# Bursts of two P·V visits between score stretches of one row half, with their sums added up on GpSimd

## The chip, the cores and the metric

The kernel runs on one core of a Trainium2 chip. The metric is device time in microseconds (us), the median of three runs; less is better. A core has TensorE (PE: matmuls, with the weight loads shown as PEld), VectorE (DVE), ScalarE (ACT), GpSimd (POOL), SyncE (SP: here it only issues DMAs) and 16 DMA engines. Matmuls write PSUM, which has 8 banks of 128 partitions x 512 fp32. GpSimd doesn't read PSUM in this kernel; ScalarE and VectorE do.

## The reference

```python
def _A_ref(x, wq, wk, wv, wo):              # S=2048, D=640, H=32 heads, Dh=20
    q = (x @ wq).reshape(B, S, H, Dh).transpose(0, 2, 1, 3)
    k = x @ wk                              # one key and value head for all
    v = x @ wv
    scores = jnp.einsum("bhqd,bkd->bhqk", q, k) * (Dh ** -0.5)
    p = softmax(scores, axis=-1)
    o = jnp.einsum("bhqk,bkd->bhqd", p, v)
    return o.transpose(0, 2, 1, 3).reshape(B, S, H * Dh) @ wo
def _B_ref(x, w1, b1, w2, b2):              # token mixing, F=1728
    h = layernorm(x, axis=-1)
    u = gelu(jnp.einsum("bsd,sf->bdf", h, w1) + b1)
    y = jnp.einsum("bdf,fs->bds", u, w2) + b2
    return y.transpose(0, 2, 1)
g = sigmoid((x * gate_w).sum(-1, keepdims=True))
return g * _A_ref(...) + (1 - g) * _B_ref(...)
```

## The kernel before

Most fp32 operands of a product are split in a high and a low part (hi, lo) in the format of the fast matmul, and a product is the sum of hi x hi, hi x lo and lo x hi.

**Attention.** 2048 queries are cut in 4 blocks of 512 and the 32 heads in 8 groups of four: 32 head groups n, each with 16 blocks of 128 keys. One unit u = (n, kb) is a head group and a key block; there are 512. For a unit, `qk` (L625) makes four score tiles s of 128 keys x 512 queries, two of them (pr) on each half b of the array's rows (partitions 0 to 63 or 64 to 127); ScalarE's exp writes each to a tile p (L635). The visit `pv_mm` (L653) then multiplies the unit's four p tiles with the values: four matmuls in four column groups of 32, all 128 rows, summed over the 16 key blocks in one bank o that belongs to a head group. Row 20 of each column group is the sum of p, since v has a column of ones. When the last key block is in, o is transposed, scaled by the inverse of the sums, transposed back (VectorE and GpSimd, the list `later`, one step per phase) and split in hi and lo for o_scr in DRAM.

The exp needs each query's maximum beforehand. So the scores are made a second time with the queries on the partitions: `ms_next` (L454) gives 64 matmuls ms per head group, each with a reduce over 512 keys on VectorE (L469). The maxima go through DRAM (`store_max`, `fetch_max`) into two more rows of the q tile qst. ms reads a q tile of its own, qmx, with the same data; both come from q_scr with six DMAs each (`load_q`).

**Fills.** Everything else of TensorE is put beside it as matmuls of 64 rows x 320 columns into one bank g: W1 of the mixer with its Gelu (`b1_jobs`, L867), W2 (`b2_jobs`, L704), and the output projection of the first eight row tiles (`a_jobs`, L816); the projection of the last eight (L773) fills the end. The weights of W1 and W2 come in chunks of 512 rows x 128: a load on SyncE, then on GpSimd a cast to hi and a subtraction to lo (`w1_upto`, L123 and L124).

**The loop.** In phase k of 488, the row half b = k % 2 gets four s (units k-1 and k) and three or four ms, alternating; the other half gets a batch of fills (9.6 on average with W1, 10.1 with W2, 7 or 8 or 15 in the projection) and at times one ms. `beside` puts the two halves' matmuls in one order by their modelled length, so that the two halves of the array work side by side. Then comes the visit of unit k-1, which needs all rows. W1 takes 180 phases, W2 256, the projection 52. Because the next phase's fills go to the same bank g from the other row half, they wait for a one-element memset on VectorE (`signal`, L645) that follows the last fill. The last 24 units run in `stretch` (L981), with two visits after one another.

Banks in the loop: three for ms (ps_m), three for s (ps_s), one for o (ps_o), one for g (ps_g). The order on each engine is the order in which the program calls the instructions; nothing reorders them.

Of the kernel before, what the change touches and what calls it, by code (L numbers as in the profile page):

```python
# [37 lines left out]
def mix_kernel(ctx: ExitStack, tc: tile.TileContext, A_x, A_wq, A_wk, A_wv, A_wo,  # L38
# [13 lines left out]
    m_scr = dram.tile([NU, P, 32], F32, name="m_scr")  # L52

    ident = const.tile([P, P], F32, name="ident")
    make_identity(nc, ident)
# [19 lines left out]
    qp = ctx.enter_context(tc.tile_pool(name="qp", bufs=2, side="right"))  # L75
# [53 lines left out]
    def load_q(n, name):  # L129
        t = qp.tile([P, 2, NB], F32R, name=name)  # L130
        qb, g = divmod(n, NQ)
        cols = slice(qb * NB, (qb + 1) * NB)

        def part(b, j, src):
            o = 64 * b + DH * j
            rows = q_scr[src, g * 4 * DH:(g + 1) * 4 * DH, cols]
            nc.sync.dma_start(out=f32(t[o:o + DH]), in_=rows.rearrange("(a b d) q -> b d a q", a=2, b=2)[b])
# [9 lines left out]
    qtiles, qmax = {}, {}  # L147
    one_by_one, q_parts_due = [False], []

    def new_q(n):  # L150
        if n < NU:
            qtiles[n] = load_q(n, "qst")

    def new_qmax(n):
        if n < NU and n not in qmax:
            qmax[n] = load_q(n, "qmx")
# [9 lines left out]
    with tc.tile_pool(name="pa", bufs=1) as pa, \  # L166
            tc.tile_pool(name="tmp", bufs=2) as tmp, \
            tc.tile_pool(name="paw", bufs=2) as paw, \
            tc.tile_pool(name="pxt", bufs=2) as pxt, \
            tc.tile_pool(name="psa", bufs=4, space=PSUM) as psa, \  # L170
            tc.tile_pool(name="pst", bufs=4, space=PSUM) as pst:
        xin = [pa.tile([P, 4, D], F32, name=name) for name in ("xa", "xb")]
# [93 lines left out]
        def x_tiles(sb, c):  # L266
            if sb < 3 and c < 4:
                xT[sb, c] = [spare(sb, c, lo) for lo in range(2)]
            elif sb == 3 and c < 3:
                pair = qp.tile([P, 2, NB], F32R, name=("qst", "qst", "qmx")[c])  # L270
# [118 lines left out]
        for sb in range(NQB):  # L389
# [11 lines left out]
            for m in range(DC):  # L401
# [23 lines left out]
                if sb == 3 and m == 1:  # L425
                    w1_upto(4)
                    new_qmax(0)
# [14 lines left out]
    pp_pool = ctx.enter_context(tc.tile_pool(name="pp", bufs=12))  # L442
    ev = ctx.enter_context(tc.tile_pool(name="ev", bufs=1))
    ps_m = ctx.enter_context(tc.tile_pool(name="ps_m", bufs=3, space=PSUM))
# [4 lines left out]
    row_max = {}  # L449
# [4 lines left out]
    def ms_next(b):  # L454
        k = given[b]
        if k >= 32 * NU:
# [5 lines left out]
        def step():  # L462
            if n not in mtiles:
                mtiles[n] = mpool.tile([P, 16, 4], F32, name="mp")
            ms = ps_m.tile([P, NB], F32, name="ms")
            nc.tensor.matmul(ms, qmax[n][64 * b:64 * b + 60, pr, qt * P:(qt + 1) * P],  # L466
# [4 lines left out]
            if min(issued) == 32 * n + 1:  # L471
                new_qmax(n + 1)
# [13 lines left out]

    def store_max(n):
        mn = row_max[n]
        mt = mpool.tile([P, 32], F32, name="mt")
# [65 lines left out]
    with tc.tile_pool(name="psb", bufs=2, space=PSUM, side="right") as psb:  # L555
# [8 lines left out]
        for fc in range(PRO):  # L564
            pu = [psb.tile([P, NB], F32, name=f"pu{r}") for r in range(2)]
            for hf in range(4):
# [16 lines left out]
                if fc == 1 and hf == 0:  # L583
                    new_q(0)
# [8 lines left out]
    ps_s = ctx.enter_context(tc.tile_pool(name="ps_s", bufs=3, space=PSUM))  # L593
    ps_o = ctx.enter_context(tc.tile_pool(name="ps_o", bufs=1, space=PSUM))
# [7 lines left out]
    def second():  # L602
        right.close()
        pools["rows"] = ctx.enter_context(tc.tile_pool(name="rows", bufs=3, side="right"))

# [17 lines left out]
    odd_s = [0]  # L623

    def qk(u, pr, b):  # L625
        n, kb = units[u]
        if kb == 4 and pr == 0 and b == 0:
            new_q(n + 1)
        q = qtiles[n]
        odd_s[0] ^= 1  # L630
        s = ps_m.tile([P, NB], F32, name="ms") if spare[0] and odd_s[0] and not loaded else ps_s.tile([P, NB], F32, name="s")
# [18 lines left out]
    otile = {}  # L650
    later = []

    def pv_mm(u):  # L653
        n, kb = units[u]
        if kb == 0:
            otile[0] = ps_o.tile([P, NB], F32, name="o")
        o = otile[0]
        for hh in range(4):
            nc.tensor.matmul(o[32 * hh:32 * hh + 32, :], v_sb[:, kb, :], ptiles.pop((u, hh)),  # L659
                             start=(kb == 0), stop=(kb == NS - 1), skip_group_check=True)  # L660
        if kb == NS - 1:
            qb, g = divmod(n, NQ)
            ot = ev.tile([P, NB // 32, 32], F32, name="ot")
            rl = ev.tile([P, NB // 32], F32, name="rl")
            on = ev.tile([P, NB], F32, name="on")
            oh = ev.tile([P, NB], F32R, name="oh")
            ol = ev.tile([P, NB], F32R, name="ol")
            nc.vector.transpose(ot.rearrange("p c e -> p (c e)"), o)

            def scale():  # L670
                nc.vector.reciprocal(rl, ot[:, :, DH])
                (nc.vector if spare[0] else nc.gpsimd).tensor_mul(ot, ot, rl[:, :, None].to_broadcast([P, NB // 32, 32]))

            def back():
                nc.vector.transpose(on, ot.rearrange("p c e -> p (c e)"))

            def high():
                osplit[:] = [oh, ol]
                if n < NU - 1:
                    nc.gpsimd.tensor_copy(oh, on)  # L680
                else:
                    nc.scalar.activation(oh, on, AF.Copy)

            def low():
                (nc.vector if n == NU - 1 else nc.gpsimd).tensor_sub(ol, on, f32(oh))
                for j, t in enumerate((oh, ol) if n < NU - 1 else ()):
                    for hh in range(4):
                        r = (4 * g + hh) * DH
                        nc.sync.dma_start(out=o_scr[j, r:r + DH, qb * NB:(qb + 1) * NB],
                                          in_=f32(t[32 * hh:32 * hh + DH, :]))  # L690

            later.extend((None, scale, back, high, low))

    def b2_jobs(st):
# [22 lines left out]
        def steps(d):  # L717
            full = [[(fc, k), (fc, k)] for fc in range(FC - 1) for k in range(3)]
            return [[lambda fc=fc, k=k, h=h: mm(fc, k, d, h) for h, (fc, k) in enumerate(f)]
                    for f in full + [[(FC - 1, 0), (FC - 1, 1)], [(FC - 1, 2)]]]  # L720
# [41 lines left out]
    def tail_job(n):  # L762
# [4 lines left out]
        def mm(c, k, d, h, first, last):  # L767
            if first:
                acc[d, h] = (ps_g.tile([P, NB], F32, name="g") if h and not d
                             else ps_m.tile([P, NB], F32, name="ms"))  # L770
# [82 lines left out]
    def b1_jobs(d, fc):  # L853
# [19 lines left out]
        return load, [([[lambda h=h, st=st, k=k: mm(st, k, h) for h in range(2)]  # L873
# [16 lines left out]
    k_tail = len(units) - TAIL  # L890
    todo = [divmod(i, FC) for i in range(PRO, 2 * FC)]
    seq = batches([b1_jobs(*t) for t in todo], [5] * len(todo))
    for i, (steps, rest, done) in enumerate(seq):
        item, j = divmod(i + 1, 5)
        rest.insert(0, lambda c=4 * (PRO + item) + (48 * j // 5) // 12: w1_upto(c + 4))
    b2 = [b2_jobs(st) for st in range(NS)]
    m = len(seq)
    seq += batches(b2, [4] * 2 * NS)
    for st in range(NS - 1):
        for j, n in ((1, 1), (2, 2), (3, 4)):  # L900
            seq[m + 8 * st + 4 + j][1].append(lambda c=W2 + 4 * (st + 1) + n: w1_upto(c))
    seq[-1][1].append(second)
    for c in range(DC):
        seq[m + 9 + 8 * c][1].append(lambda c=c: load_wo(c))
        seq[m + 11 + 8 * c][1].append(lambda c=c: split_wo(c))
    aj = [a_jobs(st) for st in range(NS - 8)]
    seq[-8][1].append(aj[0][0])
    twice = k_tail // 2 - len(seq) - 2 * len(aj)
    seq += batches(aj, [2 if i < twice else 1 for i in range(2 * len(aj))])
    ph = [(rows[1 - b], rest if b else [], done if b else []) for rows, rest, done in seq for b in range(2)]  # L910
    assert len(ph) == k_tail
    for i, k in enumerate((443, 451, 459, 467, 473, 477, 481, 485)):
        ph[k][1].append(lambda i=i: tail_load(i))

    X_US, F_US = 0.232, 0.147

    def beside(rows0, rows64, x):
# [143 lines left out]
```

## Time and profile before

| | |
|---|---|
| median of 3 runs | 1698.87 us (1698.53 to 1698.98) |
| profiled execution, span | 1697.4 us |
| DMA | 135.45 MB, 80 GB/s on average |

Busy time of the engines in stretches of 85 us, one of each stage of the loop:

| stage (window, us) | PE | DVE | ACT | POOL | reduces in it |
|---|---|---|---|---|---|
| W1 (340 to 425) | 85.00 | 76.01 | 63.50 | 37.49 | 117 |
| W2 (850 to 935) | 85.00 | 74.88 | 61.46 | 19.23 | 117 |
| projection (1445 to 1530) | 84.96 | 75.28 | 63.80 | 12.37 | 116 |

How to read it: a busy PE only says that some matmul was under way, since matmuls are pipelined and two row halves run at once. What tells is the distance between the starts of neighbouring matmuls. Of the other engines, busy time against the window's length says how far each is from setting the pace; the rows of groups give the busy time, the mean duration of one, and what its engine waited for before.

### The profile page before, as it was taken

How to read it: one execution, taken by the hardware profiler on the slowest of the kernel's cores; microseconds unless marked ns; L12 is line 12 of the kernel's file. 1: busy time of each engine (PE TensorE's matmuls, PEld its weight loads, DVE VectorE, ACT ScalarE, POOL GpSimd, SP SyncE). 2: the span in 40 equal slices, each digit the busy share in tenths (PEclk: the TensorE clock that was granted, in tenths of full speed). 3: DMA queues.
4: the chain of work that ended last, by engine and by line, in shares of the span. 5: the costliest groups of instructions: out<-in, count | busy, mean ns of one | idle time of the engine just before them, and what ended most of it. 6: DMA issues, size and time to landing. Idle time of an engine off the chain costs nothing.

```text
span 1697.4 us, 39056 instructions
## 1 busy us (share of the span) xinstructions
PE 1690.2 (100%) x14865; PEld 1103.0 (65%) x14865; DVE 1435.0 (85%) x2915; ACT 1189.8 (70%) x2322; POOL 570.4 (34%) x723
## 2 busy tenths in 40 slices
PE   9999999999999999999999999999999999999998
PEld 7899766666666666666666666666666666555666
DVE  6679898888888888888888888888888888888734
ACT  4445677777777777777777777777777777777775
POOL 6467644544445454322222212222221111111200
PEclk9999999999999999999999999999999999999999
DMA  7665322222222222121112222212111222344411
GB/s 212 192 177 147 94 64 69 65 64 64 60 69 70 70 70 69 50 64 52 57 49 70 70 60 62 63 56 61 52 52 35 62 63 64 92 113 144 132 57 57
DMA packets 173377, 135.45 MB, mean 80 GB/s; under 512 B 32729, under 2 KB 139382, under 8 KB 173190
## 3 DMA queue, kind: packets, MB, share of 16 engines
q1 hardware_dynamic: 172902, 132.63, 28.0%
q8 instruction: 117, 1.92, 0.5%
q14 instruction: 70, 0.57, 0.1%
q10 hardware_dynamic: 288, 0.33, 0.1%
HBM read 100.27 MB, written 31.65 MB: 78 GB/s over the span
## 4 chain that ended last, share of the span: by engine, by line
PE 96%; issue 2%; DVE 1%; SPq 1%; DMA 0%; POOL 0%; ACT 0%; POOLq 0%; DVEq 0%; ACTq 0%
PE o L659 30%; PE s L632 18%; PE ms L466 17%; PE g L704 12%; PE g L867 8%; PE pp L293 4%; PE pu L576 4%; PE g L816 2%; PE ms L773 1%; PE pt L285 0%; DVE mp L469 0%; PE g L773 0%; DVE st L226 0%; SPq L190 0%; SPq L188 0%
## 5 line engine op out<-in xcount | busy, mean ns | idle before, releaser
L469 DVE TENSOR_REDUCE mp<-ms 128x1 f32<-128x512 f32 x2048 | 1278.4, 684 | 171.1 <-PE ms L466 164.5
L635 ACT ACTIVATE p<-s 128x512 f32<-128x512 f32 x2048 | 1069.1, 603 | 397.4 <-PE s L632 393.8
L466 PE MATMUL ms<-kst,qmx 60*128 60x512 f32 x2048 | 846.8, 421 | 0.9 <-DVE mp L469 0.7
L632 PE MATMUL s<-qst,kst 62*128 62x512 f32 x2048 | 745.1, 404 | 0.0
L659 PE MATMUL o<-p,v_sb 128*32 128x512 f32 x4096 | 554.7, 604 | 0.0
L466 PEld LDWEIGHTS ms<-kst,qmx 60*128 60x128 f32 x2048 | 378.3, 185 | 213.6 <-DVE flag L645 181.1
L632 PEld LDWEIGHTS s<-qst,kst 62*128 62x128 f32 x2048 | 378.2, 186 | 11.5 <-issue 10.9
L867 PE MATMUL g<-slot,wh 64*128 64x320 f32 x1152 | 281.4, 318 | 0.0
L124 POOL TENSOR_TENSOR wl<-wr,wh 128x512 fp32r<-128x512 f32 (+1 forms) x176 | 219.9, 1251 | 35.8 <-ACT wh L121 21.3
L867 PEld LDWEIGHTS g<-slot,wh 64*128 64x128 f32 x1152 | 190.6, 184 | 59.8 <-DVE flag L645 59.8
L123 POOL CAST wh<-wr 128x512 fp32r<-128x512 f32 (+1 forms) x136 | 79.8, 587 | 444.4 <-PE g L704 281.7
L704 PE MATMUL g<-slot,wh 64*128 64x320 f32 x864 | 208.9, 317 | 0.0
L704 PE MATMUL g<-u,wh 64*128 64x320 f32 x864 | 208.8, 317 | 0.0
L659 PEld LDWEIGHTS o<-p,v_sb 128*32 128x32 f32 x4096 | 93.6, 108 | 137.7 <-issue 130.4
L867 PE MATMUL g<-slot,wl 64*128 64x320 f32 x576 | 179.4, 311 | 0.0
L704 PEld LDWEIGHTS g<-slot,wh 64*128 64x128 f32 x864 | 142.3, 184 | 40.2 <-DVE flag L645 40.2
L704 PEld LDWEIGHTS g<-u,wh 64*128 64x128 f32 x864 | 142.3, 184 | 40.2 <-DVE flag L645 40.2
L704 PE MATMUL g<-slot,wl 64*128 64x320 f32 x432 | 135.0, 313 | 0.0
L704 PE MATMUL g<-u,wl 64*128 64x320 f32 x432 | 134.9, 313 | 0.0
L867 PEld LDWEIGHTS g<-slot,wl 64*128 64x128 f32 x576 | 106.1, 184 | 15.1 <-DVE flag L645 15.1
L704 PEld LDWEIGHTS g<-slot,wl 64*128 64x128 f32 x432 | 79.6, 184 | 13.4 <-DVE flag L645 13.4
L704 PEld LDWEIGHTS g<-u,wl 64*128 64x128 f32 x432 | 79.5, 184 | 13.4 <-DVE flag L645 13.4
(195 smaller groups left out, 1404.0 us busy)
## 6 DMA issues: line engine op xcount, KB each, us to landing
wr<-in_B_w_dram SPq DMA_DIRECT2D x152, 256.0 KB
qmx<-q_scr SPq DMA_DIRECT2D x192, 80.0 KB
qst<-q_scr SPq DMA_DIRECT2D x192, 80.0 KB
y_scr<-yo SPq DMA_DIRECT2D x16, 320.0 KB
slot<-o_scr SPq DMA_DIRECT2D x16, 320.0 KB
o_scr<-oh SPq DMA_DIRECT2D x124, 40.0 KB
o_scr<-ol SPq DMA_DIRECT2D x124, 40.0 KB
q_scr<-qh SPq DMA_DIRECT2D x19, 256.0 KB
```

The costliest lines, as they stand in the source:

```text
L123: nc.gpsimd.tensor_copy(wh, wr)
L124: nc.gpsimd.tensor_sub(wl, wr, f32(wh))
L293: nc.tensor.matmul(pp, w, t, start=first and n == 0, stop=not more and n == len(steps) - 1)
L466: nc.tensor.matmul(ms, qmax[n][64 * b:64 * b + 60, pr, qt * P:(qt + 1) * P], kst[64 * b:64 * b + 60, kq * NB:(kq + 1) * NB], start=True, s ...
L469: nc.vector.tensor_reduce(mtiles[n][:, c, kq:kq + 1], ms, axis=AX.X, op=ALU.max)
L576: nc.tensor.matmul(pu[r][:, :HD2], w[rows, c, :], h[rows, st, :], start=(st == 0 and k == 0), stop=(st == NS - 1 and k == 2))
L632: nc.tensor.matmul(s, kst[64 * b:64 * b + 62, kb * P:(kb + 1) * P], q[64 * b:64 * b + 62, pr, :], start=True, stop=True)
L635: nc.scalar.activation(p, s, AF.Exp, scale=SCALE)
L659: nc.tensor.matmul(o[32 * hh:32 * hh + 32, :], v_sb[:, kb, :], ptiles.pop((u, hh)), start=(kb == 0), stop=(kb == NS - 1), skip_group_check ...
L704: other_tile(half, nc.tensor.matmul(hold["p"][:, :HD2], w[r, fc % HS, :], u[d][r, fc, :], start=(hold["n"] == 1), stop=(hold["n"] == 6 * F ...
L816: other_tile(half, nc.tensor.matmul(hold["p"][:, :HD2], o[r, c, :], w[r, c, d * HD2:(d + 1) * HD2], start=(hold["n"] == 1), stop=(hold["n" ...
L867: other_tile(half, nc.tensor.matmul(hold["p"][:, :HD2], w[r, st % HS, :], h[d][r, st, :], start=(hold["n"] == 1), stop=(hold["n"] == 6 * NS)))
```

## The change

- **Stretches and bursts.** The 488 phases become 244 stretches. A stretch has eight s of one row half (four units, two tiles each), about eight ms, and a batch of fills on the other half that is twice a phase's or more (24 with W1, 20 or 21 with W2, 7, 8 or 15 in the projection: W1 and W2 tiles are cut in 2 batches instead of 5 and 4). After each stretch comes one burst: the visits of two units back to back, summed in one bank. W1 takes 72 stretches, W2 128, the projection 44.
- **The sum over key blocks.** A burst's bank is copied out by ScalarE: the first of a head group into osum, the others into part (one buffer), which GpSimd adds to osum. There are eight bursts to a head group.
- **Normalising.** For all head groups but the last two, the row of sums goes from osum to DRAM and back as 128 x 16, is inverted on VectorE, goes to DRAM again and comes back spread over the partitions (rb); GpSimd multiplies and splits. One step per stretch. The last two head groups are transposed as before.
- **Banks.** s, ms and burst sums share seven banks. Which bank a matmul gets, and when it stands in the order, is worked out as the program is built, by constants for each kind of work and modelled clocks of VectorE and ScalarE (`begins`, `issue`, `arrange`, `burst`): of the two halves the one that can begin first goes next, in the bank that is free first.
- **One ring of three q tiles** serves s and ms; new_q is called at the end of every eighth stretch. The p tiles are 16 instead of 12.
- **Weight chunks** are split right after the stretch that uses the chunk four before them for the last time. Smaller edits move ident and the pools of the first stage.

```diff
+    def ring(order):
+        turns[0] += 1
+        return bank(order[turns[0] % len(order)])
...
     def ms_next(b):
         k = given[b]
-        if k >= 32 * NU:
+        if k >= 32 * NU or k // 32 not in qtiles:
...
-    def pv_mm(u):
+    def pv_mm(u, o, first, last):
+        for hh in range(4):
+            nc.tensor.matmul(o[32 * hh:32 * hh + 32, :], v_sb[:, units[u][1], :], ptiles.pop((u, hh)),
+                             start=first, stop=last, skip_group_check=True)
...
+    def collect(u, o):
         n, kb = units[u]
-        if kb == 0:
-            otile[0] = ps_o.tile([P, NB], F32, name="o")
...
+        if kb == 1:
+            osum[n] = sums.tile([P, NB], F32, name="osum")
+            nc.scalar.activation(osum[n], o, AF.Copy)
+        else:
+            part = ev.tile([P, NB], F32, name="part")
+            nc.scalar.activation(part, o, AF.Copy)
+            nc.gpsimd.tensor_add(osum[n], osum[n], part)
         if kb == NS - 1:
...
+            later.extend(norm_steps(n))
+
+    def norm_steps(n):
...
+        def rows_out():
+            nc.sync.dma_start(out=l_scr[n], in_=t.rearrange("(h r) q -> h r q", r=32)[:, DH, :])
+            nc.sync.dma_start(out=ls, in_=l_scr[n].rearrange("h (c e) -> (h c) e", e=NB // 32))
+
+        def inverse():
+            nc.vector.reciprocal(ls, ls)
+            nc.sync.dma_start(out=r_scr[n].rearrange("h (c e) -> (h c) e", e=NB // 32), in_=ls)
+            for hh in range(4):
+                nc.sync.dma_start(out=rb[32 * hh:32 * hh + 32, :], in_=r_scr[n][hh:hh + 1, :].to_broadcast([32, NB]))
+
+        def scale():
+            nc.gpsimd.tensor_mul(t, t, rb)
+
+        def high():
+            nc.gpsimd.tensor_copy(hi, t)
+
+        def low():
+            nc.gpsimd.tensor_sub(lo, t, f32(hi))
+            put_o(n, (hi, lo))
...
-    seq = batches([b1_jobs(*t) for t in todo], [5] * len(todo))
+    seq = batches([b1_jobs(*t) for t in todo], [2] * len(todo))
...
-    seq += batches(b2, [4] * 2 * NS)
+    seq += batches([b2_jobs(st) for st in range(NS)], [2] * 2 * NS)
...
+    for c in range(4 * PRO + 4, len(chunks)):
+        ph[last_use[c - 4]][1].append(lambda c=c: w1_upto(c + 1))
...
+    X_US, F_US, O_US = 0.235, 0.147, 0.858
+    W_US, FIRST_US, NEXT_US, SEEN_US = 0.11, 0.1, 0.13, 0.43
+    EACH = {"dve": (0.6, 0.74), "act": (0.48, 0.66)}
...
+    def begins(h, kind):
+        at = max(lane[h] + W_US * fresh[h], state["at"])
+        return max(at, state["f"] if kind == "f" else min(free))
+
+    def issue(h, kind, f):
+        at = state["at"] = begins(h, kind)
+        fresh[h] = False
+        lane[h] = at + (F_US if kind == "f" else X_US)
+        if kind == "f":
+            f()
+        else:
+            i = min(range(7), key=lambda i: free[i])
+            each, hold = EACH["act" if kind == "s" else "dve"]
+            free[i] = spend("act" if kind == "s" else "dve", each, at + SEEN_US) - each + hold
+            f(i)
...
+    def burst(us):
+        i = min(range(7), key=lambda i: free[i])
+        t = max(max(lane) + FIRST_US, free[i]) + len(us) * O_US
+        o = bank(i)
+        for u in us:
+            pv_mm(u, o, u == us[0], u == us[-1])
+            fetch_at(u)
+        collect(us[-1], o)
+        each, hold = EACH["act"]
+        free[i] = spend("act", each, t + 0.2) - each + hold
+        lane[:] = [t + NEXT_US] * 2
+        fresh[:] = [True, True]
...
+    for j in range(n_st):
+        h, i = j % 2, j // 2
+        ss = [lambda at, u=u, pr=pr: qk(u, pr, h, at) for u in range(4 * i, 4 * i + 4) for pr in range(2)]
+        fs, rest, done = ph[j]
+        to = owed + wants[j]
+        own = round((to + F_US / X_US * len(fs) - len(ss)) / 2)
+        if h:
+            own = (given[0] - given[1] + to + 1) // 2
...
+        arrange(h, ss, *ms, fs, done)
+        if j % 8 == 7:
+            new_q(j // 8 + 3)
+        store_maxima()
         ms_done()
         spare[0] = len(row_max) == NU
-        settle(k)
+        settle()
+        pop_chain()
         for f in rest:
             f()
...
+        if j:
+            burst((2 * j - 2, 2 * j - 1))
```

More of the change, by code (lines that the diff above doesn't have):

```diff
@@ L151, in new_q @@
         if n < NU:
[L152 to L156, printed above, removed]
+            qtiles[n] = load_q(n)
     ALL = {mybir.EngineType.PE, mybir.EngineType.DVE, mybir.EngineType.Activation, mybir.EngineType.Pool,
@@ L649, in mix_kernel @@
     osplit = []
-    otile = {}
+    osum = {}
     later = []
-    def pv_mm(u):
-        n, kb = units[u]
-        if kb == 0:
-            otile[0] = ps_o.tile([P, NB], F32, name="o")
[L657 to L660, printed above, removed]
-        if kb == NS - 1:
[L662 to L692, printed above, removed]
@@ L694, in b2_jobs, with of_chunk @@
+    def of_chunk(c, f):
+        f.chunk = c
+        return f
     def b2_jobs(st):
@@ L1001, in mix_kernel @@
+        visit(u0 - 2)
+        visit(u0 - 1)
+    for i in range(TAIL // 2):
+        stretch(i)
+    visit(len(units) - 2)
+    visit(len(units) - 1)
     accs = {}
```

286 lines of the change are left out of this document (179 added, 107 removed).

## The prediction

> **What bounds the kernel now.** I read the page first: the shares by engine, the granted clock, the chain that ended last, the costliest groups.
>
> ```profile
> span 1697.4 us, 39056 instructions
> PE 1690.2 (100%) x14865; PEld 1103.0 (65%) x14865; DVE 1435.0 (85%) x2915; ACT 1189.8 (70%) x2322; POOL 570.4 (34%) x723
> PEclk9999999999999999999999999999999999999999
> PE 96%; issue 2%; DVE 1%; SPq 1%; DMA 0%; POOL 0%; ACT 0%; POOLq 0%; DVEq 0%; ACTq 0%
> L469 DVE TENSOR_REDUCE mp<-ms 128x1 f32<-128x512 f32 x2048 | 1278.4, 684 | 171.1 <-PE ms L466 164.5
> L635 ACT ACTIVATE p<-s 128x512 f32<-128x512 f32 x2048 | 1069.1, 603 | 397.4 <-PE s L632 393.8
> ```
>
> The chain is TensorE for 96% of the span at full clock, and the two engines that empty its banks sit idle mostly for its score matmuls. VectorE at 85% is the next bound. So the question is what TensorE spends per phase, and whether VectorE and ScalarE can follow when that shrinks. The first and last starts of the fill matmuls give the stages:
>
> ```profile
> L867 PE MATMUL g<-slot,wh x1152: 300/305/418, 179.4 to 702.1; 64*128 64x320 f32 x192
> L704 PE MATMUL g<-u,wh x864: 300/305/418, 703.8 to 1430.7; 64*128 64x320 f32 x173
> L816 PE MATMUL g<-slot x480: 299/306/415, 1455.8 to 1613.3; 64*128 64x320 f32 x160
> L773 PE MATMUL ms<-slot,u x180: 299/306/409, 1614.8 to 1654.1; 64*128 64x320 f32 x180
> ```
>
> By the code the W1 stage has 180 phases, the W2 stage 256, the projection stage 52. So a phase takes (703.8 - 179.4) / 180 = 2.913 us, (1455.8 - 703.8) / 256 = 2.938 and (1614.8 - 1455.8) / 52 = 3.058; the loop takes 1435.4 us, and this is what the change rebuilds. One phase of the W2 stage in the timeline:
>
> ```profile
> 1000.28 0.50 PE L466 MATMUL ms<-kst,qmx 60*128 60x512 f32 x1
> 1000.53 0.30 PE L704 MATMUL g<-u,wh 64*128 64x320 f32 x1
> 1000.62 0.40 PE L632 MATMUL s<-qst,kst 62*128 62x512 f32 x1
> ...
> 1000.81 2.50 DVE L469 TENSOR_REDUCE mp<-ms 128x1 f32<-128x512 f32 x4 [0.28 <-PE ms L466]
> ...
> 1001.11 2.06 ACT L635 ACTIVATE p<-s 128x512 f32<-128x512 f32 x4 [0.89 <-PE s L632]
> ...
> 1001.70 0.30 PE L704 MATMUL g<-u,wl 64*128 64x320 f32 x1
> ...
> 1001.79 0.47 PE L632 MATMUL s<-qst,kst 62*128 62x512 f32 x1
> ...
> 1002.19 1.10 PE L659 MATMUL o<-p,v_sb 128*32 128x512 f32 x8
> 1002.64 0.06 DVE L645 MEMSET flag<- 1x1 f32 x1
> ```
>
> What the reader is to see. The two row halves run beside each other. In the score half 6 score matmuls (s or ms) start from 1000.62 to 1001.79: **0.235 us each**. In the other half 9 fills start from 1000.53 to 1001.70: **0.147 us each**. The first matmul after a visit lasts 0.50 us against 0.39, because no weights were loaded ahead: **0.11 us**. A bank is seen by its reader about 0.53 us after the first matmul starts (1000.28 to 1000.81). A reduce costs (2.50 - 0.684) / 3 = **0.60 us** in a row, an exp (2.06 - 0.603) / 3 = **0.487 us**. The price of a visit, alone and in a pair, stands at the end of the loop:
>
> ```profile
> 1606.06 0.48 PE L632 MATMUL s<-qst,kst 62*128 62x512 f32 x1
> 1606.19 0.60 PE L816 MATMUL g<-slot 64*128 64x320 f32 x3
> 1606.72 1.06 PE L659 MATMUL o<-p,v_sb 128*32 128x512 f32 x8
> 1607.71 0.50 PE L466 MATMUL ms<-kst,qmx 60*128 60x512 f32 x1
> ...
> 1621.40 1.92 PE L659 MATMUL o<-p,v_sb 128*32 128x512 f32 x16
> 1623.26 0.50 PE L632 MATMUL s<-qst,kst 62*128 62x512 f32 x2
> ```
>
> The last fill ends its turn at 1606.19 + 3 x 0.147 = 1606.63, the visit starts 0.09 later, and the next matmul 0.99 us after that. Two visits in a row take 1.86 us. So a visit is 0.87 us of work and 0.12 + 0.09 + 0.11 = **0.32 us of switching**, paid 487 times.
>
> The model of a phase is then 0.11 + longer half + 0.09 + 0.99. W1: 7 x 0.235 = 1.645 beside 0.235 + 9.6 x 0.147 = 1.646, so 2.84 (measured 2.913). W2: 0.235 + 10.125 x 0.147 = 1.72, so 2.91 (2.938). Projection: 40 phases with 7 or 8 fills and 12 with 15, mean 2.96 (3.058). It comes out 0.03 to 0.1 us short of a phase; I add **0.05 us** to each new stretch.
>
> **The change, part by part.** *Bursts.* 488 phases become 244 stretches and 487 visits become 243 bursts. With 0.32 us saved per pair this alone is worth 78 us. Against it a stretch must be worked out anew, since its banks and its readers are pushed harder.
>
> W1 stage, 72 stretches: 24 fills beside 8 s and 8 ms in the other half (a ninth ms in every third, put among the fills). Longer half 16 x 0.235 = 3.76; stretch 0.11 + 3.76 + 0.09 + 1.86 = **5.82 us**. W2, 128 stretches: 20.25 fills and 2 ms beside 14 score matmuls: 0.47 + 2.98 = 3.45; **5.51 us**. Projection, 44 stretches: 15.45 score matmuls and 7.5 or 15 fills; if TensorE alone set it, the halves shared evenly would be 2.4 or 2.9, so 4.4 to 5.0 us.
>
> *Seven banks.* These must hold. A bank is in use from its matmul to the end of its reader: 0.54 after the stretch opens the first reduce or exp starts; a bank comes back 0.71 us (reduce) or 0.63 (exp) later. The 0.71 is from here, where TensorE waits for a reduce that began at 1503.69 and lasts 0.684:
>
> ```profile
> 1503.69 2.47 DVE L469 TENSOR_REDUCE mp<-ms 128x1 f32<-128x512 f32 x4
> ...
> 1504.40 0.18 PEld L466 LDWEIGHTS ms<-kst,qmx 60*128 60x128 f32 x1 [0.31 <-DVE mp L469]
> ```
>
> So banks return at 1.25, 1.85, 2.45, 3.05, 3.65 from VectorE and at 1.17, 1.66, 2.14, 2.63, 3.12, 3.61 from ScalarE. With 16 score matmuls and one bank for the burst, 10 of 17 must be back before the burst starts: the tenth is 3.61, and the W2 stretch reaches its burst at 0.11 + 3.45 + 0.09 = 3.65. It fits, with nothing to spare. W1 reaches it at 3.96. Projection needs 9.45 of them: between 3.12 and 3.61, at 3.34, so banks set that stage: 3.34 + 1.86 = **5.20 us**.
>
> *Readers.* VectorE: 8 reduces from 0.54 on end at 5.4; the flag that lets the next stretch's fills begin stands behind them, at 5.5, and the fills begin at 5.51 + 0.11 or later. In W1 with nine ms 6.1, against 5.82 + 0.11 + 0.235 = 6.17. Covered; each 0.1 us more of VectorE work per stretch would cost 24 us. Its transposes and one reciprocal per head group go, 1.42 us in eight stretches:
>
> ```profile
> L668 DVE STREAM_TRANSPOSE ot<-o 128x512 f32<-128x512 f32 x32 | 22.9, 717 | 3.2 <-PE o L659 3.2
> L675 DVE STREAM_TRANSPOSE on<-ot 128x512 f32<-128x512 f32 x32 | 22.5, 702 | 0.1
> L308 ACT ACTIVATE qh<-pp 128x512 fp32r<-128x512 f32 x19 | 11.2, 590 | 13.5 <-PE pp L293 7.6 <-issue 2.9 <-DMA kst<-k_hi 1.5
> L672 POOL TENSOR_TENSOR ot<-ot,rl 128x512 f32<-128x512 f32 x30 | 31.5, 1050 | 141.3 <-DVE rl L671 141.3
> ```
>
> ScalarE gets 243 copies out of a bank, same form as L308: 0.59 us alone, 0.487 in a row, 118 us in all. A copy waits for the burst's end, and the 8 exps of the next stretch are queued behind it; it starts about when the burst's 1.86 us are over and ends before the first new bank is readable 0.54 later, so I cost it at nothing; without that cover it is up to 0.59 x 243 = 143 us. 8 exps, the copy and a quarter of an eviction are 4.6 us of 5.5.
>
> *GpSimd sums.* 212 adds of L672's form, 1.05 us each. The copy also waits for the previous add (one buffer "part"). GpSimd in W1:
>
> ```profile
> 510.00:595.00 85.00, 85.00 (x751) 52.99 (x752) 75.74 (x156) 63.44 (x126) 40.27 (x53) 1.00 0.27 70
> ```
>
> 40.27 of 85 us, so 13.8 per ten phases of one W1 tile. The same tile now takes four stretches of 5.87: 13.8 + 4 x 1.05 = 18 of 23.5 us. It holds, but the weight splits of two chunks come together at the end of every second stretch, ahead of that burst's add. Cost taken: nothing; from above, the rival below.
>
> *Norm through DRAM.* Per head group SyncE gets 7 issues more (sums out and in, inverse out, four broadcasts in) and loses 6 with the second q tile: even. Two of them wait for a landing, and weight loads, y stores and the fetch of the maxima queue behind them; VectorE's reciprocal comes a stretch after its load, GpSimd's scaling a stretch after its broadcasts, so each has most of a 5.5 us stretch of cover. Taken as nothing; with the cover gone, each 1 us that a load is late costs 31 us.
>
> *One ring of q.* The six loads of a tile are issued at the end of every eighth stretch behind a y store; these rows are the nearest:
>
> ```profile
> 844.57 0.33 SPq L715 DMA_DIRECT2D y_scr<-yo  x1
> ...
> 846.08 2.40 SPq L137 DMA_DIRECT2D qst<-q_scr  x6
> ```
>
> Three parts (1.2 us to issue) are needed some 4.5 us after the burst starts. That is about what store, issue and transfer take: 0 to 1 us late, 30 times; at most 30 us, taken as nothing.
>
> *Sum.* 72 x 5.87 + 128 x 5.56 + 44 x 5.25 = 422.6 + 711.7 + 231.0 = 1365 us (the missing first burst and the slow start cancel). 1435.4 - 1365 = 70 us. The end has one visit more and a lone phase less, 1 us. Span 1697.4 - 71 = 1626; the median lies 1.5 us above the profiled span, so **1628 us**. For the range: without the 0.05, 12 us less; projection at TensorE's 4.4 to 5.0, 23 us less, and I take the larger of the two, not both; q tiles, norm loads and late copies together 60 us more.
>
> **Rivals.** *GpSimd late.* After a W1 stretch with splits it has a scaling (1.05), two splits (3.7) and the add (1.05) before the next copy may start 5.87 us later, 5.8 in all, and a Gelu step of 1.3 fits no more. If 36 such stretches run 1.24 us late, 45 us: **1673**. For it: the tight sum, one buffer. Against: the scaling comes once in eight stretches, GpSimd is a quarter idle.
>
> *Reduce banks set the pace (the slower side).* TensorE takes banks in a fixed order. If exps come late (behind a copy, an eviction, a Gelu step), ms in effect turn over three banks: the eighth ms needs the fifth reduce back, 3.65, loads its weights unhidden and runs, 0.11 + 0.235, and the burst starts at 4.09: 5.95 in W2, 6.15 in W1, 5.62 in projection, with 0.05 each 446 + 767 + 249 = 1463, so 27 us over today's loop: **1725**. It decides once an exp is 0.4 us late in most stretches. For it: 3.61 against 3.65, and VectorE already waited on at 1504.40. Against: ScalarE has 0.9 us to spare per stretch, and a late exp is often replaced by the next reduce at 3.65.
>
> *Banks never bind:* TensorE's halves set projection too, 23 us less: **1605**. For it: the wait at 1504.40 is short. Against: 16 score matmuls in a stretch against 8 in a phase, on one bank more.
>
> *The clock drops.* Waits for banks in every stretch could lower the granted clock; here it is 9 in all 40 slices, the 0.31 us bank wait among them. A tenth of the loop at half clock would be 137 us more: **1765**. The Trainium skill (TensorE: Matmul & The Clock Gate, A second HAM failure mode: psum-queue depth-cycling) says that idling between groups while banks are cycled makes the clock gate oscillate; by that rule this is what the shared banks would do, and this trace does not show it.
>
> **How the numbers follow.** Forecast 0.70, GpSimd late 0.10, banks never bind 0.04, reduce banks 0.13, clock 0.02, a wash 0.01. Less than 0.2% (3.4 us) can't be told from no change. Faster: 0.70 + 0.10 + 0.04 = 0.84; slower 0.14; same 0.02. The range goes from the lower bound, 1604, to 1628 + 60 = 1688, past the late GpSimd; slower reduces and the clock, 0.15, lie outside.
>
> **What would show it.** Two-visit bursts of 1.86 us from start to next matmul, and stretches of 5.8 to 5.9, 5.5 to 5.6 and 5.2 to 5.3 us by stage; projection slower per phase than TensorE's halves, with TensorE waiting on exps and reduces there alone. VectorE over 85% and its idle time in front of reduces about 0.5 us per stretch. ScalarE's copies waiting for TensorE, not for GpSimd. If reduces show next to no idle time, or TensorE's waits on them exceed 50 us, the slower rival holds; copies that wait on GpSimd's add for over 20 us show the other; a PEclk digit under 9 the last. Stretches beyond 5.88 us on average would make the forecast of any gain wrong.

## The result, and the profile after

The changed kernel takes 1741.66 us (median of four runs, 1740.68 to 1743.69) beside 1698.92 us before: ratio 1.025, 95% interval 1.024 to 1.027. It is slower by 43 us, where 1628 us was forecast. The profiled execution has a span of 1739.4 us. From its page, the span, the busy times, the clock, the chain that ended last, and the groups of reduces, exps, adds and copies (mean ns of one behind the comma):

```profile
span 1739.4 us, 39303 instructions
PE 1678.5 (96%) x14865; PEld 1143.1 (66%) x14865; DVE 1378.2 (79%) x2612; ACT 1283.1 (74%) x2565; POOL 843.9 (49%) x935
PE 73%; ACT 8%; POOL 5%; DMA 4%; issue 4%; DVE 3%; SPq 3%; POOLq 0%; ACTq 0%; DVEq 0%
L477 DVE TENSOR_REDUCE mp<-x 128x1 f32<-128x512 f32 x2048 | 1259.0, 683 | 273.2 <-PE x L474 186.9
L642 ACT ACTIVATE p<-x 128x512 f32<-128x512 f32 x2048 | 1034.4, 636 | 29.9 <-PE x L639 24.7
L680 POOL TENSOR_TENSOR osum<-osum,part 128x512 f32<-128x512 f32 x212 | 272.7, 1286 | 421.4 <-ACT part L679 415.3
L679 ACT ACTIVATE part<-x 128x512 f32<-128x512 f32 x212 | 126.8, 598 | 267.8 <-PE x L662 187.4
```

No engine beside TensorE is near its limit: VectorE fell from 85% to 79%, GpSimd is half idle. And TensorE's share of the chain fell from 96% to 73%, and GpSimd, DMA, ScalarE and SyncE's queue, which had about 1% between them, have 20%. A chain that changes engine so often speaks of delays that are handed on. An ordinary stretch of the W2 stage in the timeline, from its first score matmuls to the next stretch's:

```profile
900.08 0.50 PE L639 MATMUL x<-q,kst 62*128 62x512 f32 x1
900.27 0.60 ACT L679 ACTIVATE part<-x 128x512 f32<-128x512 f32 x1 [0.71 <-PE x L662]
900.65 4.88 DVE L477 TENSOR_REDUCE mp<-x 128x1 f32<-128x512 f32 x8 [0.88 <-PE x L639]
900.77 4.02 ACT L642 ACTIVATE p<-x 128x512 f32<-128x512 f32 x8
...
903.86 0.16 PEld L662 LDWEIGHTS x<-p,v_sb 128*32 128x32 f32 x8 [0.30 <-ACT p L642]
903.86 1.92 PE L662 MATMUL x<-p,v_sb 128*32 128x512 f32 x16
...
905.72 0.18 PEld L474 LDWEIGHTS x<-kst,q 60*128 60x128 f32 x1 [0.84 <-DVE flag L652]
```

The burst takes 905.72 - 903.86 = 1.86 us, the stretch 905.72 - 900.08 = 5.64: about as forecast (5.56). So I took the distance between the starts of neighbouring bursts for all stretches, and sorted them by their place in a head group (eight stretches; place = j mod 8):

| stage (stretches measured) | forecast each | median | places far from it (mean) | sum, us | forecast sum |
|---|---|---|---|---|---|
| W1 (70) | 5.87 | 5.92 | place 5: 8.53 (9 stretches) | 441.2 | 410.9 |
| W2 (128) | 5.56 | 5.72 | place 0: 6.78, place 1: 7.82 (16 each) | 777.8 | 711.7 |
| projection (44) | 5.25 | 5.59 | place 0: 6.16 (6) | 246.0 | 231.0 |

Most stretches are near the forecast; a few in each head group are 0.6 to 2.6 us late. What engines waited for, in the whole execution (total us, times, longest):

```profile
POOL wh L123 <- DMA wr<-in_B_w_dram: 82.2, 14, 6.7
ACT part L679 <- POOL osum L680: 75.0, 23, 4.2
POOL osum L701 <- DMA rb<-r_scr: 71.2, 22, 4.6
PEld x L662 <- ACT p L642: 56.6, 195, 0.7
PE x L474 <- DMA q<-q_scr: 15.7, 12, 2.3
```

23 copies waited for GpSimd's add, which the prediction named as the sign of its late-GpSimd rival; and GpSimd waited for loads. Here are places 0 and 1 of a W2 head group in the timeline (the SPq rows are SyncE's issues):

```profile
677.89 0.70 ACT L769 ACTIVATE yo<-g,b2g,og_half 128x320 f32<-128x320 f32 x1
678.61 0.34 SPq L772 DMA_DIRECT2D y_scr<-yo  x1
679.07 2.52 SPq L137 DMA_DIRECT2D q<-q_scr  x6
681.68 0.36 SPq L105 DMA_DIRECT2D wr<-in_B_w_dram  x1
682.09 1.16 SPq L109 DMA_DIRECT2D wr<-in_B_w_dram  x2
683.55 0.47 PE L474 MATMUL x<-kst,q 60*128 60x512 f32 x1 [1.60 <-DMA q<-q_scr]
684.57 3.61 PE L662 MATMUL x<-p,v_sb 128*32 128x512 f32 x16
685.85 0.40 POOL L123 CAST wh<-wr 128x256 fp32r<-128x256 f32 x1 [6.46 <-DMA wr<-in_B_w_dram]
687.01 1.27 POOL L680 TENSOR_TENSOR osum<-osum,part 128x512 f32<-128x512 f32 x1
688.31 0.60 ACT L679 ACTIVATE part<-x 128x512 f32<-128x512 f32 x1 [3.42 <-POOL osum L680]
688.64 4.88 DVE L477 TENSOR_REDUCE mp<-x 128x1 f32<-128x512 f32 x8 [2.69 <-PE x L639]
688.81 4.02 ACT L642 ACTIVATE p<-x 128x512 f32<-128x512 f32 x8
```

Read it from the top. The y store stands at the head of SyncE's queue and waits for the last eviction of the W2 tile (677.89 to 678.59). The q loads stand behind it, and TensorE waits 1.60 us for q. Behind those stands the load of the tile's last raw chunk; GpSimd waits 6.46 us for it, and the add of the burst sum behind that split starts 1.16 us after it at 687.01. The add is the only reader of the one buffer part, so ScalarE's next copy waits, and the eight exps queued behind the copy with it.

In W1 the late place 5 has another train on GpSimd: at 408.88 the scaling, then two splits, then the add at 413.97; the copy that waits for it holds the exps:

```profile
403.67 1.73 SPq L698 DMA_DIRECT2D rb<-r_scr  x4
...
408.88 1.29 POOL L701 TENSOR_TENSOR osum<-osum,rb 128x512 f32<-128x512 f32 x1
410.11 0.61 POOL L123 CAST wh<-wr 128x512 fp32r<-128x512 f32 x1
410.81 1.29 POOL L124 TENSOR_TENSOR wl<-wr,wh 128x512 fp32r<-128x512 f32 x1
412.04 0.61 POOL L123 CAST wh<-wr 128x512 fp32r<-128x512 f32 x1
412.73 1.28 POOL L124 TENSOR_TENSOR wl<-wr,wh 128x512 fp32r<-128x512 f32 x1
413.97 1.28 POOL L680 TENSOR_TENSOR osum<-osum,part 128x512 f32<-128x512 f32 x1
...
415.28 0.60 ACT L679 ACTIVATE part<-x 128x512 f32<-128x512 f32 x1 [2.76 <-POOL osum L680]
```

One thing more: the burst at 684.57 lasts 3.61 us instead of 1.92. The view of windows shows the granted clock (the column before the last two) in that time, and in the 3.41 us before and after:

```profile
681.25:684.66 3.41, 1.81 (x20) 1.30 (x22) 2.11 (x4) 2.44 (x6) 0.00 (x0) 1.00 0.53 139
684.66:688.08 3.42, 3.42 (x16) 0.51 (x16) 1.29 (x4) 0.23 (x1) 2.15 (x3) 0.50 0.51 150
688.08:691.49 3.41, 3.41 (x39) 3.24 (x36) 2.85 (x5) 3.18 (x7) 1.48 (x2) 1.00 0.02 5
```

TensorE was busy for 1.81 of 3.41 us, and for the next 3.41 us it had half its clock. There are eight such pieces in the loop, one of 6.83 us and seven of 3.41: 30.7 us at 0.50, so at most 15.4 us of the loss. The digits of the page's PEclk line, all 9, do not show them.

### The profile page after: what moved, and what is told of

Same layout as the page of the kernel before. It is cut to its first block, busy times and chain, and to the rows that moved or that the text cites. A ratio compares the mean times of both kernels' runs of the same rounds, so it can differ in the third digit from the quotient of the medians.

```text
span 1739.4 us, 39303 instructions
## 1 busy us (share of the span) xinstructions
PE 1678.5 (96%) x14865; PEld 1143.1 (66%) x14865; DVE 1378.2 (79%) x2612; ACT 1283.1 (74%) x2565; POOL 843.9 (49%) x935
## 3 DMA queue, kind: packets, MB, share of 16 engines
q8 instruction: 117, 1.92, 0.5%
## 4 chain that ended last, share of the span: by engine, by line
PE 73%; ACT 8%; POOL 5%; DMA 4%; issue 4%; DVE 3%; SPq 3%; POOLq 0%; ACTq 0%; DVEq 0%
PE x L662 24%; PE x L474 14%; PE x L639 14%; ACT p L642 6%; PE g L761 6%; PE g L923 5%; PE pp L291 4%; PE pu L587 3%; DVE mp L477 2%; DMA wr<-in_B_w_dram 2%; POOL osum L680 2%; PE g L872 1%; SPq L137 1%; POOL wl L124 1%; ACT part L679 1%
## 5 line engine op out<-in xcount | busy, mean ns | idle before, releaser
L477 DVE TENSOR_REDUCE mp<-x 128x1 f32<-128x512 f32 x2048 | 1259.0, 683 | 273.2 <-PE x L474 186.9
L642 ACT ACTIVATE p<-x 128x512 f32<-128x512 f32 x2048 | 1034.4, 636 | 29.9 <-PE x L639 24.7
L474 PE MATMUL x<-kst,q 60*128 60x512 f32 x2048 | 800.7, 426 | 25.8 <-DMA q<-q_scr 15.7
L639 PE MATMUL x<-q,kst 62*128 62x512 f32 x2048 | 774.3, 416 | 28.6 <-ACT part L679 20.3
L662 PE MATMUL x<-p,v_sb 128*32 128x512 f32 x4096 | 496.1, 602 | 0.0
L639 PEld LDWEIGHTS x<-q,kst 62*128 62x128 f32 x2048 | 362.1, 186 | 180.3 <-issue 44.4
L680 POOL TENSOR_TENSOR osum<-osum,part 128x512 f32<-128x512 f32 x212 | 272.7, 1286 | 421.4 <-ACT part L679 415.3
L474 PEld LDWEIGHTS x<-kst,q 60*128 60x128 f32 x2048 | 375.0, 186 | 154.2 <-DVE flag L652 39.4
L679 ACT ACTIVATE part<-x 128x512 f32<-128x512 f32 x212 | 126.8, 598 | 267.8 <-PE x L662 187.4
L662 PEld LDWEIGHTS x<-p,v_sb 128*32 128x32 f32 x4096 | 107.4, 109 | 228.9 <-issue 170.3
L123 POOL CAST wh<-wr 128x512 fp32r<-128x512 f32 (+1 forms) x136 | 79.9, 588 | 97.5 <-DMA wr<-in_B_w_dram 82.2
```

What stands on the lines that cost most here:

```text
L123: nc.gpsimd.tensor_copy(wh, wr)
L474: nc.tensor.matmul(ms, qtiles[n][64 * b:64 * b + 60, pr, qt * P:(qt + 1) * P], kst[64 * b:64 * b + 60, kq * NB:(kq + 1) * NB], start=True, ...
L477: nc.vector.tensor_reduce(mtiles[n][:, c, kq:kq + 1], ms, axis=AX.X, op=ALU.max)
L639: nc.tensor.matmul(s, kst[64 * b:64 * b + 62, kb * P:(kb + 1) * P], q[64 * b:64 * b + 62, pr, :], start=True, stop=True)
L642: nc.scalar.activation(p, s, AF.Exp, scale=SCALE)
L662: nc.tensor.matmul(o[32 * hh:32 * hh + 32, :], v_sb[:, units[u][1], :], ptiles.pop((u, hh)), start=first, stop=last, skip_group_check=True)
```

## The experiments

Times are medians, with ratios to the kernel before on the same chip (1699.2 to 1699.5 us). The theory: three deliveries per head group are late (the q tile, the last raw chunk, the adds in W1 behind normalising and splits), and each is passed on to TensorE, two of them through part. The rivals: banks or readers are too slow throughout, or GpSimd as a whole is. The first four runs change one thing each.

**e1: two buffers for part** (halves is a pool of two; one tile of the last head groups is moved into it, for room).

```diff
-            part = ev.tile([P, NB], F32, name="part")
+            part = halves.tile([P, NB], F32, name="part")
```

> Two buffers for part instead of one, nothing else (the last head group's low half moves to one of them). Theory, GpSimd late: once or twice per head group GpSimd stands still for a weight chunk's load or for the broadcast inverses, the add of the last burst stands behind that, part is not free, ScalarE's copy waits (75 us in all on osum's add) and the eight exps behind it come late. A second buffer lets the copy go ahead: the stretches 1 after a multiple of 8 in W2 fall from 7.8 us to about 5.7 (16 x 2.1 = 34 us), those 5 after it in W1 from 8.5 by about half, since the Gelu's tanh still waits for GpSimd (12 us); in all about 1697 us. Rival, banks: the shared banks set the pace in every stretch, and the late copies are only where it shows; then the time stays within 10 us of 1742.

Measured: 1710.61 us, ratio 1.008 (1.006 to 1.010). W2's place 1 falls from 7.82 to 5.66 us and no other place in that stage moves by more than 0.07 us. GpSimd waits for the load as long as before:

```profile
POOL wh L123 <- DMA wr<-in_B_w_dram: 89.5, 15, 6.9
POOL osum L702 <- DMA rb<-r_scr: 70.3, 23, 4.6
ACT yo L531 <- POOL yo L544: 16.1, 10, 2.5
```

The wait stays, its path to TensorE is gone: 16 x 2.16 = 35 us of W2. W1's place 5 stays at 8.60, so there the second buffer alone doesn't do it: as the last row shows, ScalarE's tanh step, with exps queued behind it, now waits for a Gelu step (yo) that stands behind the same train on GpSimd (16.1 us in all, against 7.6 us in the changed kernel).

**e2: a fourth buffer for raw weights**, so that a chunk's load is issued one split earlier.

```diff
-    w1r = right.enter_context(tc.tile_pool(name="w1r", bufs=3, side="right"))
+    w1r = right.enter_context(tc.tile_pool(name="w1r", bufs=4, side="right"))
-            w1_load(c + 3)
+            w1_load(c + (4 if c >= 4 * PRO else 3))
```

> Four buffers for raw weight chunks and each loaded one chunk earlier; nothing else. Theory, GpSimd late: in W2 the load that GpSimd waits for (82 us on it, 14 times) is issued only after a split in the same stretch and behind the y store and the six q loads; one chunk earlier it has landed. W2 stretches 1 after a multiple of 8 fall from 7.8 to about 5.7: 34 us less, about 1708 us; W1 and the late q tile unchanged. Rival, one buffer of part with a GpSimd that is simply too full: taking away the load wait only moves the queue, under 10 us less.

Measured: 1711.2 us, ratio 1.008 (1.006 to 1.011). Place 1 falls to 5.74. GpSimd's wait for the load (82.2 us in the changed kernel) is gone, and the copies wait 16.2 us for adds instead of 75.0. So two different edits, one at the cause and one on the path, remove the same loss.

**e3: the q loads ahead of the y store.**

```diff
-                nc.sync.dma_start(out=y_scr[st * P:(st + 1) * P, :], in_=t)
+                late_stores.append(lambda t=t: nc.sync.dma_start(out=y_scr[st * P:(st + 1) * P, :], in_=t))
...
             new_q(j // 8 + 3)
+        while late_stores:
+            late_stores.pop(0)()
```

> The y store is issued after the q loads of the same stretch, not before; nothing else. Theory: the W2 stretches at multiples of 8 (6.8 us against 5.7 for the others) wait for the new q tile, whose loads stand behind a store that waits 1.2 us for ScalarE's eviction; without it they fall to about 5.7, 17 us less, and the weight load behind them is issued 1 us earlier, 10 to 16 us less: about 1712 us. Rival: the q loads are late because of their own issue and transfer, not the store before them: under 5 us less.

Measured: 1702.15 us, ratio 1.002 (1.001 to 1.004), 10 us more than expected. SyncE in the same head group:

```profile
675.25 2.46 SPq L137 DMA_DIRECT2D q<-q_scr  x6
677.81 0.35 SPq L773 DMA_DIRECT2D y_scr<-yo  x1
678.26 0.37 SPq L105 DMA_DIRECT2D wr<-in_B_w_dram  x1
```

This run is 1.5 us ahead by then, so I count from the start of the same earlier burst (671.53 in the changed kernel, 670.04 here): the q loads go out 7.54 - 5.21 = 2.3 us earlier, since they don't wait for the eviction, and the raw chunk behind them 10.15 - 8.22 = 1.9 us, where 1 us was expected. Place 0 falls from 6.78 to 5.64 (18 us), and place 1 half-way too, to 6.74 (17 us). W1 and the projection, which the expectation left as they were, are 2.5 and 2.4 us shorter.

**e4: one step more between the broadcast of the inverse and GpSimd's scaling.**

```diff
-        return rows_out, inverse, scale, high, low
+        return rows_out, inverse, None, scale, high, low
```

> GpSimd's scaling of a finished head group, its cast and its subtraction each one stretch later, in a stretch without weight splits before them in W1; nothing else. Theory, GpSimd late: in W1 the scaling waits for its broadcasts, the two splits, the add and the Gelu step stand behind it, and the copy and the tanh wait. W1 stretches 5 after a multiple of 8 fall from 8.5 to about 6: 9 x 2.5 = 22 us less, about 1719 us, W2 unchanged within 5 us. Rival: GpSimd's work in that stretch is too much wherever the scaling stands: under 8 us less.

Measured: 1722.64 us, ratio 1.014 (1.009 to 1.019). W1's place 5 falls from 8.53 to 6.85; W2 is unchanged (777.8 and 780.0).

**e7: W1's two splits one stretch apart.**

```diff
-        ph[last_use[c - 4]][1].append(lambda c=c: w1_upto(c + 1))
+        ph[last_use[c - 4] + (c % 2 if c < W2 else 0)][1].append(lambda c=c: w1_upto(c + 1))
```

> The changed kernel with the two weight splits that come together at the end of every second W1 stretch put one stretch apart (one split of 1.9 us per stretch); nothing else. Theory (in W1 the add is late because scaling, two splits and add stand in one row on GpSimd): in stretch 5 of eight the add comes 1.9 us earlier, nine times, 17 us, and stretch 1 of eight loses its excess of 0.35 us, nine times, 3 us: 1742 - 20 = 1722 us, all of it in the W1 stage. Rival (only the late landing of the inverse of the sums holds that stretch, and GpSimd waits for it in any case): within 5 us of 1742.

Measured: 1723.87 us, ratio 1.014 (1.012 to 1.017). Place 5 falls to 6.50, all of the gain in W1. Place 1, 6.26 in the changed kernel, stays at 6.25: the two splits are not what makes it 0.4 us long. The rival, a late landing of the inverse, has the changed kernel's trace against it: in four of W1's eight scalings GpSimd waited for no DMA (that at 408.88 is one), and the place-5 stretches behind these took 8.36 to 10.57 us; behind the four with such a wait they took 6.81 to 8.81. So W1's loss hangs on the length of the train on GpSimd: taking out either the scaling or a split relieves it.

**e5: e2, e3 and e4 together. e6: e1, e3 and e4 together. e8: e1, e3, e4 and e7 together.**

> The changed kernel with a fourth buffer for raw weights, the q loads ahead of the y store, and the steps of the normalising spread by one more stretch; part stays one buffer. Theory (the loss sits in three kinds of stretch per head group, each late for a reason of its own): W2 stretches 0 and 1 of eight come to 5.64 as their neighbours, so the W2 stage falls from 777.8 to about 725 us, and W1's stretch 5 of eight to about 6.85 as with the normalising alone, stage 441 to 424: 1742 - 53 - 17 = 1672 us, faster than the kernel before. Rival (one shared cause, GpSimd as a whole is too slow, so what is gained in one place is given back in the next): the three single gains, 20 to 40 us each, do not add up and the time stays near that of the best single edit, 1700 us.

> As the run before it, but with two buffers for part in place of the fourth buffer for raw weights. Theory: W2's stretch 1 of eight is cured by either, since the wait is passed on to the burst only through the one buffer; and the second buffer also lets ScalarE go on in W1 while GpSimd is at its splits: W2 stage 725, W1 stage under 424, in all 1660 to 1672 us. Rival (GpSimd as a whole too slow): about 1700 us.

> Two buffers for part, the q loads ahead of the y store, the normalising spread by one more stretch and the weight splits of W1 one stretch apart. Theory: no stretch of W1 or W2 is held by GpSimd or by a load any more, W1 stage 70 x 5.9 = 413 us, W2 725, projection 244: 1742 - 28 - 53 - 2 = 1659 us; what is left over the forecast of 1628 is 0.06 to 0.09 us in each ordinary stretch, 0.25 in the projection's, and the first and last stretches. Rival (GpSimd as a whole too slow): no faster than the run with two buffers, q loads and normalising by more than 2 us.

Measured: e5 1666.91 us, ratio 0.981 (0.980 to 0.983); e6 1665.80 us, 0.980 (0.979 to 0.982); e8 1660.50 us, 0.977 (0.976 to 0.979). So the change does make the kernel faster, by 39 us, once the deliveries are on time. In e8 the places named above are 6.25 (W1, place 5), 5.64 and 5.66 (W2, places 0 and 1), and the chain runs through TensorE and ScalarE, without GpSimd, DMA or SyncE's queue. From its page and its waits:

```profile
PE 88%; ACT 8%; issue 3%; DVE 1%; POOL 0%; POOLq 0%; ACTq 0%; DVEq 0%
L682 POOL TENSOR_TENSOR osum<-osum,part 128x512 f32<-128x512 f32 x212 | 273.9, 1292 | 454.1 <-ACT part L681 445.4
PEld x L664 <- ACT p L643: 60.8, 213, 0.4
```

GpSimd does the same adds for the same 1.29 us each: it was never too slow as a whole, which ends that rival. The wait left is that of the bursts for a bank from an exp, 0.29 us in 213 of them; how much of it costs time this run doesn't show.

**e9: e8 without the copies into part and their adds.**

```diff
-            part = halves.tile([P, NB], F32, name="part")
-            nc.scalar.activation(part, o, AF.Copy)
-            nc.gpsimd.tensor_add(osum[n], osum[n], part)
+            pass
```

> The fastest kernel so far (1660.5 us) without the copies into part and their adds: 212 of 243 burst sums are left out of the result; the order of all else is the same. Theory (the copy, which I cost at nothing, holds the eight exps of the next stretch back by 0.16 us, from 0.54 to 0.70 us after its first matmul, and the burst at the end waits for a bank from an exp): W2's ordinary stretch falls from 5.64 to 5.55 us or a little less, the stage from 724 to about 713, the projection stage from 241.5 to about 235; W1, which TensorE itself paces, by under 4 us: in all 1640 to 1646 us. Rival (the ordinary stretch is 0.08 us over the forecast because of the reduces or of TensorE's own order): no stage falls by more than 2 us, 1657 or more.

Measured: 1639.80 us, ratio 0.965 (0.962 to 0.968). W2 falls from 723.8 to 712.5 us, W1 from 418.7 to 410.5, the projection only from 241.5 to 240.4. An ordinary stretch of e8, then one of e9:

```profile
911.04 0.49 PE L475 MATMUL x<-kst,q 60*128 60x512 f32 x1
911.24 0.60 ACT L681 ACTIVATE part<-x 128x512 f32<-128x512 f32 x1 [1.12 <-PE x L664]
911.74 4.02 ACT L643 ACTIVATE p<-x 128x512 f32<-128x512 f32 x8
...
914.83 1.06 PE L664 MATMUL x<-p,v_sb 128*32 128x512 f32 x8
```

```profile
898.02 0.50 PE L475 MATMUL x<-kst,q 60*128 60x512 f32 x1
898.59 4.03 ACT L643 ACTIVATE p<-x 128x512 f32<-128x512 f32 x8 [1.50 <-PE x L640]
...
901.69 1.92 PE L664 MATMUL x<-p,v_sb 128*32 128x512 f32 x16
```

With the copy the exps begin 0.70 us after the first matmul, without it 0.57; the burst comes after 3.79 and 3.67 us. So the copy costs W2 0.09 us per stretch. W1 lost 8 us, not under 4: most of it is at places 1 and 5, from 6.25 to 5.87 us (17 x 0.38 = 6.5), where ScalarE has steps of a Gelu to do beside the copy. That the copy does it, and not the adds that GpSimd is spared too, is not shown: no run takes out one of them alone. For the projection the theory is wrong: its stretches stay 0.2 us over the forecast without the copy.

**e10: e8 with six banks in the loop.**

```diff
-        i = min(range(7), key=lambda i: free[i])
+        i = min(range(6), key=lambda i: free[i])
```

> The fastest kernel so far with six shared banks in the loop instead of seven; nothing is left out. Theory (the ordinary stretch of W2 and the projection is paced by the return of banks): each burst needs one more return before it starts, and returns come 0.27 us apart on average, so W2 and the projection lose 0.1 to 0.3 us per stretch, 17 to 52 us, and W1, which has 0.3 us to spare, up to 0.1 us, 7 us: 1680 to 1720 us. Rival (the readers' rate paces the stretch, and a bank more or less changes nothing): under 1668 us.

Measured: 1746.63 us, ratio 1.028 (1.025 to 1.031). W2 goes from 5.65 to 6.06 us per stretch, W1 from 5.98 to 6.26, the projection from 5.49 to 5.83. The direction is that of the theory, the size 27 us over its range, and W1, which was to have 0.3 us to spare, lost 0.28 us a stretch. The likely reason is that a bank less shifts not only the burst but the matmuls ahead of it too; no run tests this. Score matmuls wait for an exp 212 times, against 111 in e8. In W2 one of these and the burst both wait:

```profile
955.02 0.18 PEld L475 LDWEIGHTS x<-kst,q 60*128 60x128 f32 x1 [0.20 <-ACT p L643]
955.45 0.16 PEld L664 LDWEIGHTS x<-p,v_sb 128*32 128x32 f32 x8 [0.24 <-DVE mp L478]
```

## Why the prediction was wrong

It missed by 1741.7 - 1628 = 113.7 us. e8 divides that: 81.2 us were late deliveries and the half clock after them, which it removes, and 32.5 us remain: 7.8 over the forecast in W1 (most of it at places 1 and 5), 12.1 in W2, 10.5 in the projection and 2.1 elsewhere. The sum had the late deliveries at nothing, and the range gave them 60 us.

- **One ring of q: "0 to 1 us late, 30 times; at most 30 us, taken as nothing". This step failed.** I priced a y store by its issue (0.33 us), but its place in the queue holds everything behind it until the eviction is done, and the q tile behind it is needed at once. In W2 place 0 was 1.14 us late 16 times, 18 us. And I had not followed the queue one entry further, to the raw chunk.
- **GpSimd sums: "Cost taken: nothing". This step failed**, and it cost the most. In W2 the late raw chunk held the split, the add behind it, the one buffer, the copy and the exps: 16 x 2.2 = 35 us, which e1 and e2 each took away. I had looked for trouble in W1 alone, where GpSimd is fuller. There the rival's train of scaling, two splits, add and Gelu step is what happened, but not as 36 stretches 1.24 us late: nine were late, by 2.6 us in the mean. An add takes 1.286 us, not 1.05. The rival's 1673 us was too low by 69.
- **Norm through DRAM: "Taken as nothing". This step failed too**, in W1, and not only by the late loads that it spoke of: the scaling ends up in front of two splits, and e4 takes 9 x 1.7 = 15 us away. Together with the splits (e7) place 5 is worth 9 x 2.28 = 20.5 of the 22.5 us by which e8's W1 stage is shorter.
- **ScalarE's copies: "I cost it at nothing".** The cover was 0.16 us too short. With copies and adds out the loop is 8.2 + 11.3 + 1.1 = 20.6 us shorter. This is most of the 32.5.
- **Seven banks: "It fits, with nothing to spare".** Nearly right: one bank less costs 86 us, and without copies W2's stretch is 5.55 us. But that TensorE would wait on exps and reduces in the projection "alone" was wrong: in e9 all 128 bursts of W2 still wait for a bank from an exp. In the projection the forecast of 5.25 us met 5.49 in e8, 10.5 us over the stage; this part is open, since neither a late delivery nor the copy explains it.
- **Bursts.** Right: 1.86 us each. Ordinary stretches of 5.82 in W1 and, without copies, 5.55 in W2 are near TensorE's own 5.82 and 5.51. The slower rival (reduces set the pace) did not come: VectorE's idle time before reduces grew to 273 us. (VectorE over 85% was no good sign: its 1378.2 us would be 84.8% of the forecast span too.) The kernel was slower for another reason than the one I had on that side.
- **The clock.** A weak form of the rival: not short waits for banks in every stretch but the long pauses of the late ones were followed by half clock, for 30.7 us, at most 15.4 us of the 81. Three of the eight pieces lie in W1, in the three longest stretches at place 5 (9.57 to 10.57 us), five in W2. e8's loop shows none.

## What to carry to other kernels

A mean over a stage hides a stall that comes once per group: where one engine's queue carries stores, loads and small steps together, walk it entry by entry through the stretch in which they fall together, and charge an entry with what it waits for, not with its issue. A single buffer between a busy engine and a slack one passes every delay of the slack one on; a second buffer, or an earlier load, may be worth the whole gain. When a restructured kernel comes out slower, compare its ordinary stretch with the forecast before giving up the structure.

## What was not expected of the hardware

- The granted clock halves for one window of 3.41 us (once for two), and pauses of TensorE of 1.29 to 1.75 us were enough. Each stall of that length can so cost as much again (at most 1.7 us). Not each did: the loop has 42 pauses of over 0.5 us, of up to 2.27, and eight halved pieces. In this trace it matters how a pause falls into a fixed grid: the eight pieces start whole multiples of 3.413 us apart. In the window of that grid ahead of each, TensorE was busy for 1.67 to 1.94 us (1.81 in the row shown), and only two other windows of the loop have as little (1.81 and 1.94); the pause of 2.27 us is cut in two by the grid and halved nothing. The border isn't sharp by this measure: in e7 a window with 1.68 us busy was not followed by half clock, in e4 one with 2.22 was. The Trainium skill (TensorE: Matmul & The Clock Gate, What's actually happening) gives a free-running window of 3413 ns, which agrees, and a return to half clock after at least one idle window, where here about half a window of idle time was enough. The rule of bank cycling that the prediction cited did not show: in e8 213 of 243 bursts wait for a bank, 0.29 us each, and the mean clock of the span is 1.000. It is no hard test of the rule, since TensorE is busy for 1650.9 of e8's 1658.7 us.
- GpSimd's in-place add of two full 128x512 tiles takes 1.286 us; the multiplication by a broadcast operand (L672 before) took 1.050, that by a full tile (L701 after) 1.29. So in these rows the difference goes with the second full operand, not with the operation.
